# The last 240 columns of a weight quarter as eight loads of three rows, on a single-core decode block

## Chip, cores and metric

One core of a Trainium2 chip runs the whole kernel in one launch. The metric is the device time in microseconds; before the change it is 242.6 us, the median of three runs (242.56 to 242.74).

## What is computed

A decode step of one transformer block with adaptive layer norms, for 4 sequences of one token, D = 512, all in float32. The reference, cut:

```
mod = silu(c) @ w_mod                       # six vectors: sa, ca, ga, sb, cb, gb
h = layernorm(x) * (1 + ca) + sa
q = h @ wq                                  # 512 x 4096, 32 heads of 128
k, v = last 2048 positions of the caches    # 8 groups of kv heads
x = x + ga * (softmax(q k^T / sqrt(128)) v) @ wo
h = layernorm(x) * (1 + cb) + sb
x = x + gb * (silu(h @ w1) * (h @ w3)) @ w2     # 512 x 1792 and 1792 x 512
```

Some 101 MB of caches and weights are read once; the arithmetic for 4 tokens is small beside that.

## The kernel before

**Memory.** An SBUF tensor `ring` has three slots of 128 x 16384 floats (8.39 MB each). Each large input passes through a slot as one DMA of 128 rows of up to 65,536 bytes. All loads are issued by SP (`nc.sync`), in program order, but for `wq`, which ACT issues at the start. The order on SP: `w_mod_a` (the part of w_mod for the first norm, with x and c), `kv_in[0]` to `kv_in[6]` (keys and values of one group each), `wo_mod`, `last_k_wo`, `last_v`, `wo`, `w1`, `w3`, and `w2` in pieces. SP waits ahead of a load until the slot has been read; everything behind the waiting load waits with it.

**Stages.** First x is transposed and normalised, with four contraction quarters of `w_mod_a` (`mod_columns`, line 264), which gives `h` and its transpose `hT` (line 286). Then q (lines 291 to 296): for each half of the heads, four contraction quarters k, four column groups i, 512 columns each; the four column groups write four bands of 32 partitions of one PSUM bank. ACT scales q, PE transposes it, DVE copies it into `qT`. Then `group(g)` (line 332) for the eight groups: scores into four banks, maximum on DVE, exponential on ACT into `p_all` (the tensor `p_sb`), transposes, products with v. After g, the load for g + 3 is issued into the slot that g has left. Output projection, second norm and the feed-forward follow: gate from `w1`, up from `w3`, and `w2` in 14 chunks of 128 rows.

**The end.** `W2_CUTS` cuts w2 into pieces that land one after the other: `[0, 7, 11, 13, 14]` are pieces of 7, 4, 2 and 1 chunks. The chunks of the first piece are multiplied whole (512 columns a product, line 453) into `part`, which ACT copies to `work` (line 454); each later chunk takes eight products of 64 columns (`add_rows`, line 456), and the contents of `work` are added by eight more, ahead of the third piece.

**Waits.** There is no scheduler. Each engine works in program order. `Program.__call__` (line 50) records what each operation touches as boxes, and makes it wait for earlier operations whose boxes overlap. For an SBUF access a box is a range of partitions and a range of columns; the partitions come from lines 28 to 33, the test from lines 61 to 66:

```
    (step, parts), *free = ap.ap
    p0, lo = divmod(ap.offset, row)
    p1, hi = p0 + (parts - 1) * (step // row) + 1, lo + sum((n - 1) * s for s, n in free) + 1
...
                apart = lo >= h or l >= hi or not (writes or wrote)
                if p0 < q1 and q0 < p1 and not (apart and (not psum or other.engine == engine)):
                    if other.engine != engine or other.dma or (wrote and engine != "tensor"):
                        key = other if other.dma else other.engine
                        latest[key] = max(latest.get(key, other), other, key=lambda o: o.index)
```

A step between partitions is not kept: the box runs from the first partition to the last. An operation that touches what an earlier DMA writes waits for that DMA's own semaphore. `emit` (line 77) leaves out waits that the engine knows of already.

The functions as they stand:

Of the kernel before, what the change touches and what calls it, by code (L numbers as in the profile page):

```python
# [8 lines left out]
B, D, HQ, G, SK, DH, W, FF = 4, 512, 32, 8, 8192, 128, 2048, 1792  # L9
P = 128  # L10
R = HQ // G
NT = 4
NC = 4
CHUNKS = [(c, j) for c in range(4) for j in range(4 if c < 2 else 3)]
NF = len(CHUNKS)
W2_CUTS = [0, 7, 11, 13, 14]
EPS = 1e-5
HALF = 8192

# [123 lines left out]
                nc.sync.sem_clear(done)  # L143


def block_kernel(nc, w_mod_a, wq, kv_in, wo_mod, last_k_wo, last_v, wo, w1, w3, w2, out):

# [2 lines left out]
    do = Program(nc)  # L152

    def sb(name, *shape):
        return nc.alloc_sbuf_tensor(name, (P, *shape), F32).ap()
# [5 lines left out]
    slots = [ring[:, n * 2 * HALF : (n + 1) * 2 * HALF] for n in range(3)]  # L161
# [10 lines left out]
    def load(dst, src, cuts=(0, 1), queue="sync"):  # L172
        step = src.shape[1] // cuts[-1]
        for lo, hi in zip(cuts[:-1], cuts[1:]):
            do(queue, "dma_start", dst[:, lo * step : hi * step], src[:, lo * step : hi * step])
        return dst[:, : src.shape[1]]
# [9 lines left out]
    wq_t = load(slots[1], wq, queue="scalar")  # L186
    do("scalar", "preload_act_table_set", "natural_log_exp_and_others")
    kv = [None] * G
    kv[0] = load(slots[2], kv_in[0])

# [1 line left out]
    ident = shifted[:, 4:]  # L194
    do("gpsimd", "memset", shifted, 0.0)
    do("gpsimd", "affine_select", ident, ident, compare_op=ALU.not_equal, fill=1.0, base=0, pattern=[[-1, P]], channel_multiplier=1)
    sc = sb("sc", 4, 32)
    do("gpsimd", "memset", sc, 0.0)

# [36 lines left out]
    xc, sq, h = (sb(n, P) for n in ("xc", "sq", "h"))  # L236
    ss, ln, r0, ve, a, r = (sb(n, 1) for n in ("ss", "ln", "r0", "ve", "a", "r"))
# [19 lines left out]
    def transposed(name):  # L257
        hp = bank()[:, :P]
        do("tensor", "transpose", hp, h, ident)
        hT = sb(name, 4, 32)  # L260
        do("vector", "tensor_copy", hT.rearrange("p j i -> p (j i)"), hp)
        return hT
# [23 lines left out]
    hT = transposed("hT")  # L286
    kv[1] = load(slots[0], kv_in[1])


    work = sb("work", 512)  # L290
    for half in range(2):
        qp = s_ps[half]
        for k in range(4):
            for i in range(4):
                at = ((half * 4 + i) * 4 + k) * 512
                do("tensor", "matmul", qp[32 * i : 32 * i + 32, :], hT[:, k, :], wq_t[:, at : at + 512], start=(k == 0), stop=(k == 3))
    for half in range(2):
        do("scalar", "mul", work, s_ps[half], DH**-0.5)
        qtp = bank()
# [14 lines left out]
            do("tensor", "matmul", a_ps[32 * i : 32 * i + B, :], oT[:, g, i, :], wo_t[g][:, i, :], start=(g == 0), stop=(g == G - 1))  # L314

    mx, nm, ls, l, rl = (sb(n, m) for n, m in (("mx", NT), ("nm", 1), ("ls", NT), ("l", 1), ("rl", 1)))
    p_all = sb("p_sb", NT * 512)
    p_sb = [p_all[:, t * 512 : (t + 1) * 512] for t in range(NT)]
    pT = [sb(f"pT{t}", B, NC, R) for t in range(NT)]
    o_own, o_sum = sb("o_own", NC, P), sb("o_sum", P)  # L320
# [1 line left out]
    def heads_out(g):  # L322

        otp = bank()[:, : R * B]
        if g < G - 1:
            do("tensor", "matmul", otp, o_sum, pick, start=True, stop=True)
        else:
            for c in range(NC):
                do("tensor", "matmul", otp, work[:, c * P : (c + 1) * P], pick_c[:, c].rearrange("p r b -> p (r b)"), start=(c == 0), stop=(c == NC - 1))
        do("vector", "tensor_copy", oT[:, g].rearrange("p r b -> p (r b)"), otp)  # L330
# [62 lines left out]
    w3_t = load(slots[0][:, HALF:], w3)  # L393
    w2_t = load(slots[0][:, :HALF], w2, W2_CUTS)
    heads_out(G - 1)
# [54 lines left out]
    w2_t = w2_t.rearrange("p (n c) -> p n c", n=NF)  # L450
    for n in range(W2_CUTS[1]):
        i = n % 4
        do("tensor", "matmul", part[32 * i : 32 * i + 32, :], hidT[:, n, 4:], w2_t[:, n, :], start=(n < 4), stop=(n + 4 >= W2_CUTS[1]))
    do("scalar", "copy", work, part)
# [6 lines left out]

    for n in range(W2_CUTS[1], NF):
        if n == W2_CUTS[-2]:
            do.mark()
        if n == W2_CUTS[2]:

# [8 lines left out]
def _layout(i):  # L475
    import numpy as np

    def a(t):
        return np.ascontiguousarray(t)

    k = i["A_k_cache"][:, :, SK - W :, :].reshape(B, G, NT, 512, DH)
    v = i["A_v_cache"][:, :, SK - W :, :].reshape(B, G, NT, NC, P, DH)
    wm = i["w_mod"].reshape(4, P, 6, 4, P)
    xc = np.concatenate([i[n].reshape(B, 4, P).transpose(2, 1, 0).reshape(P, 16) for n in ("A_x", "c")], 1)
    w2 = i["B_w2"].reshape(14, P, D)
    wo = a(i["A_wo"].reshape(2, 4, R, P, D).transpose(0, 3, 1, 2, 4)).reshape(2, P, 8192)
    kv = np.concatenate([k.transpose(1, 4, 2, 0, 3).reshape(G, P, 8192), v.transpose(1, 4, 2, 0, 3, 5).reshape(G, P, 8192)], 2)
    return {
        "w_mod_a": np.concatenate([a(wm[:, :, :2].transpose(1, 0, 3, 2, 4)).reshape(P, 4096), xc], 1),
        "wq": a(i["A_wq"].reshape(4, P, G, 512).transpose(1, 2, 0, 3)).reshape(P, 16384),  # L490
        "kv_in": kv[: G - 1],
        "wo_mod": np.concatenate([wo[0], a(wm[:, :, 2:].transpose(1, 0, 3, 2, 4)).reshape(P, 8192)], 1),
        "last_k_wo": np.concatenate([kv[G - 1, :, :8192], wo[1, :, :4096]], 1),
        "last_v": a(kv[G - 1, :, 8192:]),
        "wo": a(wo[1, :, 4096:]),
        "w1": a(i["B_w1"].reshape(4, P, FF).transpose(1, 0, 2)).reshape(P, 4 * FF),
        "w3": a(i["B_w3"].reshape(4, P, FF).transpose(1, 0, 2)).reshape(P, 4 * FF),
        "w2": a(np.stack([w2[4 * j + c] for c, j in CHUNKS], 1)).reshape(P, NF * D),
    }
# [15 lines left out]
```

## Time and profile before

| | |
|---|---|
| median of three runs | 242.6 us |
| span of the profiled execution | 241.1 us |
| PE, DVE, ACT, POOL busy | 146.8, 55.2, 24.0, 2.6 us |
| moved by DMA | 101.38 MB, mean 421 GB/s |
| the chain that ended last | DMA 73%, PE 20% |
| SP waiting, longest | 44.4 us, before the result's store |

The page gives the profiled execution by its span, from the first to the last instruction; the runs' times are 1.5 us longer. The page's chain follows the work that ended last back to what released it. A windows row has the stretch, its length, the busy time of PE, PE's weight loads, DVE, ACT and POOL with the number of instructions, the granted clock, the DMA share and the GB/s. A DMA row gives the time from issue to landing, which includes the time that it stood in the queue.

### The profile page before, as it was taken

How to read it: one execution, taken by the hardware profiler on the slowest of the kernel's cores; microseconds unless marked ns; L12 is line 12 of the kernel's file. 1: busy time of each engine (PE TensorE's matmuls, PEld its weight loads, DVE VectorE, ACT ScalarE, POOL GpSimd, SP SyncE). 2: the span in 40 equal slices, each digit the busy share in tenths (PEclk: the TensorE clock that was granted, in tenths of full speed). 3: DMA queues.
4: the chain of work that ended last, by engine and by line, in shares of the span. 5: the costliest groups of instructions: out<-in, count | busy, mean ns of one | idle time of the engine just before them, and what ended most of it. 6: DMA issues, size and time to landing. Idle time of an engine off the chain costs nothing.

```text
span 241.1 us, 2468 instructions
## 1 busy us (share of the span) xinstructions
PE 146.8 (61%) x1103; PEld 52.8 (22%) x1103; DVE 55.2 (23%) x140; ACT 24.0 (10%) x36; POOL 2.6 (1%) x11
## 2 busy tenths in 40 slices
PE   0000169756782972945767586567296919964876
PEld 0000132213222312201311222221131202422333
DVE  4000220240303124123132124130312014103120
ACT  2000000103003003001200300300300000320100
POOL 3000000000000000000000000000000000000000
PEclk9999997995977799779797589797977997996899
DMA  8999989898989898989999999999999999999993
GB/s 316 414 436 425 500 370 500 351 511 359 511 359 503 370 502 370 489 383 478 391 479 391 478 394 468 402 468 405 457 413 424 435 405 435 407 432 426 416 415 133
DMA packets 2889, 101.38 MB, mean 421 GB/s; under 512 B 448, under 2 KB 448, under 8 KB 704
## 3 DMA queue, kind: packets, MB, share of 16 engines
q1 hardware_dynamic: 2736, 92.85, 89.5%
q10 hardware_dynamic: 144, 8.39, 8.1%
q8 instruction: 8, 0.13, 0.2%
q14 instruction: 1, 0.01, 0.0%
HBM read 101.20 MB, written 0.03 MB: 420 GB/s over the span
## 4 chain that ended last, share of the span: by engine, by line
DMA 73%; PE 20%; DVE 3%; ACT 2%; issue 0%; SPq 0%
DMA ring<-kv_in 30%; DMA ring<-wo_mod 17%; DMA ring<-w 15%; DMA ring<-w_mod_a 11%; PE s_ps L57 8%; PE bank L57 7%; PE o_ps L57 4%; PE a_ps L57 2%; ACT p_sb L57 2%; DVE nm L57 2%; DVE p_sb L57 0%; DVE e L57 0%; DVE sq L57 0%; DVE xc L57 0%; DVE tot L57 0%
## 5 line engine op out<-in xcount | busy, mean ns | idle before, releaser
L57 PE MATMUL s_ps<-ring,qT 128*32 128x512 f32 x256 | 37.0, 731 | 20.2 <-DMA ring<-kv_in 14.7
L57 PE MATMUL bank<-ident,p_sb 128*128 128x128 f32 (+1 forms) x136 | 27.4, 350 | 30.8 <-ACT p_sb L57 30.7
L57 PE MATMUL o_ps<-ring,pT 128*16 128x512 f32 x256 | 37.8, 696 | 0.0
L57 PEld LDWEIGHTS bank<-ident,p_sb 128*128 128x128 f32 (+1 forms) x136 | 19.6, 177 | 51.9 <-ACT p_sb L57 31.7
L57 ACT ACTIVATE p_sb<-s_ps,nm 128x2048 f32<-128x2048 f32 (+1 forms) x11 | 16.5, 1501 | 143.2 <-DVE oT L57 105.2
L57 DVE TENSOR_REDUCE nm<-s_ps 128x1 f32<-128x2048 f32 x7 | 16.0, 2292 | 34.5 <-PE s_ps L57 34.5
L57 DVE COPY pT<-bank 128x64 f32<-128x64 f32 x32 | 7.2, 224 | 56.1 <-PE bank L57 56.1
L57 PEld LDWEIGHTS s_ps<-ring,qT 128*32 128x32 f32 x256 | 9.0, 131 | 47.5 <-issue 20.7
L57 PE MATMUL bank<-ident,xs 128*128 128x128 f32 x1 | 0.5, 473 | 27.8 <-POOL xs L57 27.8
L57 PE MATMUL s_ps<-ring,h2T 128*32 128x512 f32 (+1 forms) x64 | 9.1, 664 | 2.3 <-DMA ring<-w 2.3
L57 PE MATMUL a_ps<-ring,oT 128*4 128x512 f32 x64 | 9.1, 709 | 2.0 <-DMA ring<-wo_mod 2.0
L57 PE MATMUL s_ps<-ring,hT 128*32 128x512 f32 x64 | 8.8, 711 | 0.4 <-DVE hT L57 0.4
L57 PEld LDWEIGHTS o_ps<-ring,pT 128*16 128x16 f32 x256 | 5.4, 98 | 11.6 <-issue 9.2
L57 DVE SCALAR_TENSOR_TENSOR o_own<-o_ps,rl,own 128x512 f32<-128x512 f32 x7 | 5.3, 751 | 11.1 <-PE o_ps L57 11.1
L57 DVE TENSOR_REDUCE o_sum<-o_own 128x128 f32<-128x512 f32 x7 | 7.2, 1029 | 0.2
L57 PE MATMUL bank<-ring,sc 128*32 128x256 f32 (+1 forms) x64 | 7.2, 610 | 0.0
L57 PEld LDWEIGHTS bank<-ident,xs 128*128 128x128 f32 x1 | 0.2, 180 | 27.8 <-POOL xs L57 27.8
L57 DVE TENSOR_SCALAR e<-e 128x16 f32<-128x16 f32 x1 | 0.2, 174 | 23.8 <-ACT e L57 23.8
L57 DVE TENSOR_REDUCE mx<-s_ps 128x1 f32<-128x512 f32 x4 | 2.8, 691 | 7.6 <-PE s_ps L57 7.6
L57 DVE COPY qT<-bank 128x64 f32<-128x64 f32 x8 | 2.2, 277 | 9.8 <-PE bank L57 9.4
L57 PEld LDWEIGHTS s_ps<-ring,h2T 128*32 128x32 f32 x64 | 2.6, 129 | 7.4 <-issue 4.5
L57 PE MATMUL s_ps<-ring,hidT 128*32 128x64 f32 (+1 forms) x126 | 3.7, 262 | 0.3 <-DVE hidT L57 0.3
(93 smaller groups left out, 55.4 us busy)
## 6 DMA issues: line engine op xcount, KB each, us to landing
ring<-w SPq DMA_DIRECT2D x2, 3584.0 KB, 38.3
ring<-last_k_wo SPq DMA_DIRECT2D x1, 6144.0 KB, 30.5
ring<-last_v SPq DMA_DIRECT2D x1, 4096.0 KB, 39.9
ring<-w_mod_a SPq DMA_DIRECT2D x1, 2064.0 KB, 26.6
ring<-wo SPq DMA_DIRECT2D x1, 2048.0 KB, 43.4
ring<-w SPq DMA_DIRECT2D x1, 1792.0 KB, 40.9
ring<-w SPq DMA_DIRECT2D x1, 1024.0 KB, 42.9
ring<-w SPq DMA_DIRECT2D x1, 512.0 KB, 43.7
```

The source lines that it names most:

```text
L57: op = Op(engine, lambda: getattr(getattr(self.nc, engine), method)(*args, **kw), [])
```

## The change

The last 240 columns of the last 512-column block of `wq` (the last contraction quarter of the last column group) are left out of the `wq` load, whose rows shrink from 65,536 to 64,576 bytes. The 128 x 240 values come in instead as 24 rows of 1440 floats, an input `guests`, into partitions 0 to 11 and 32 to 43 of `p_sb`. Eight DMAs on SP carry them, each three rows with a step of four partitions, 5760 bytes a row. POOL first clears 44 partitions of `p_sb`. The eight stand on SP behind `w_mod_a` and ahead of `kv_in[0]`.

To use them, PE makes six copies of columns of `hT` with the rows shifted to partitions 0 to 43 (products of `h` with a part of the identity, into a bank that DVE copies to `hg`), and six products of 240 columns add to the last block of q ahead of its own, which is now 272 columns wide. `p_sb` is allocated earlier for this; its other uses come later.

Apart from that, w2's first piece has 8 chunks instead of 7, the second 3 instead of 4.

The diff, without the host's part beyond the input that it adds:

```
-W2_CUTS = [0, 7, 11, 13, 14]
+W2_CUTS = [0, 8, 11, 13, 14]
+GUESTS = 240
+GUEST_AT = [(0, 0, 12), (12, 0, 12), (24, 0, 8), (64, 0, 12), (76, 0, 12), (84, 4, 12)]
...
     kv = [None] * G
-    kv[0] = load(slots[2], kv_in[0])
...
     do("gpsimd", "affine_select", ident, ident, ...
+
+    p_all = sb("p_sb", NT * 512)
+    do("gpsimd", "memset", p_all[:44], 0.0)
+    guest = p_all[:44, : 6 * GUESTS]
+    for m in range(2):
+        for c in range(4):
+            do("sync", "dma_start", guest[32 * m + c : 32 * m + 12 : 4], guests[12 * m + c : 12 * m + 12 : 4])
+    kv[0] = load(slots[2], kv_in[0])
     sc = sb("sc", 4, 32)
...
     kv[1] = load(slots[0], kv_in[1])
+    hg = p_all[:44, 6 * GUESTS :][:, : 6 * 32]
+    hp = bank()[:44, : 6 * 32]
+    for n, (at, _, _) in enumerate(GUEST_AT):
+        do("tensor", "matmul", hp[:, 32 * n : 32 * n + 32], h[:, at : at + 44], ident[:, 96:], start=True, stop=True)
+    do("vector", "tensor_copy", hg, hp)
...
                 at = ((half * 4 + i) * 4 + k) * 512
-                do("tensor", "matmul", qp[32 * i : 32 * i + 32, :], hT[:, k, :], wq_t[:, at : at + 512], start=(k == 0), stop=(k == 3))
+                n = min(512, 16384 - GUESTS - at)
+                if n < 512:
+                    for c in range(6):
+                        do("tensor", "matmul", qp[96:, n:], hg[:, 32 * c : 32 * c + 32], guest[:, c * GUESTS : (c + 1) * GUESTS], start=False, stop=False)
+                do("tensor", "matmul", qp[32 * i : 32 * i + 32, :n], hT[:, k, :], wq_t[:, at : at + n], start=(k == 0), stop=(k == 3))
...
-    p_all = sb("p_sb", NT * 512)
...
+        "wq": a(wq[:, : 16384 - GUESTS]),
+        "guests": guests.reshape(24, 6 * GUESTS),
```

What stands on SP at the program's start, before. A name with `part0` in brackets is a semaphore; the last part of it is the engine, or the number of the operation if that is a DMA.

```order
L57 DMA ring<-w_mod_a 128x4128 [waits barrier_Pool_Activation_PE_DVE_SP_release]
L57 DMA ring<-kv_in 128x16384
L57 DMA ring<-kv_in 128x16384 [waits part0_22_tensor,part0_22_vector]
L57 DMA ring<-kv_in 128x16384 [waits part0_22_tensor] x5
L57 DMA ring<-wo_mod 128x16384 [waits part0_22_tensor]
```

And after, on the same engine from the same start. The numbers 6 to 13 are the eight guest loads.

```order
L59 DMA ring<-w_mod_a 128x4128 [waits barrier_Pool_Activation_PE_DVE_SP_release]
L59 DMA p_sb<-guests 3x1440 [waits part0_30_gpsimd]
L59 DMA p_sb<-guests 3x1440 [waits part0_30_6]
L59 DMA p_sb<-guests 3x1440 [waits part0_30_7]
L59 DMA p_sb<-guests 3x1440 [waits part0_30_8]
L59 DMA p_sb<-guests 3x1440
L59 DMA p_sb<-guests 3x1440 [waits part0_30_10]
L59 DMA p_sb<-guests 3x1440 [waits part0_30_11]
L59 DMA p_sb<-guests 3x1440 [waits part0_30_12]
L59 DMA ring<-kv_in 128x16384
L59 DMA ring<-kv_in 128x16384 [waits part0_30_tensor,part0_30_vector]
```

The first `kv_in` moved from the second place to the tenth, behind eight loads of which the first waits for POOL and six for the load ahead of them.

On PE, from the transpose of `h` to the start of the first group, before:

```order
L57 MATMUL bank<-ident,h 128x128
L57 MATMUL s_ps<-ring,hT 32x512 x32
L57 MATMUL bank<-ident,work 128x128 x8
L57 MATMUL s_ps<-ring,qT 32x512 x16
L57 MATMUL bank<-ident,p_sb 128x128 x8
```

and after:

```order
L59 MATMUL bank<-ident,h 128x128
L59 MATMUL bank<-ident,h 44x32 x6
L59 MATMUL s_ps<-ring,hT 32x512 x31
L59 MATMUL s_ps<-p_sb 32x240 x6
L59 MATMUL s_ps<-ring,hT 32x272
L59 MATMUL bank<-ident,work 128x128 x8
L59 MATMUL s_ps<-ring,qT 32x512 x16
```

Six small products went in ahead of q, and six of 240 columns ahead of the last one of q.

More of the change, by code (lines that the diff above doesn't have):

```diff
@@ L143, in emit, with block_kernel @@
                 nc.sync.sem_clear(done)
-def block_kernel(nc, w_mod_a, wq, kv_in, wo_mod, last_k_wo, last_v, wo, w1, w3, w2, out):
+def block_kernel(nc, w_mod_a, wq, guests, kv_in, wo_mod, last_k_wo, last_v, wo, w1, w3, w2, out):
     do = Program(nc)
@@ L485, in _layout @@
     w2 = i["B_w2"].reshape(14, P, D)
+    wq = a(i["A_wq"].reshape(4, P, G, 512).transpose(1, 2, 0, 3)).reshape(P, 16384)
+    guests = np.zeros((2, 12, 6, GUESTS), np.float32)
+    for n, (at, lo, hi) in enumerate(GUEST_AT):
+        for m in range(2):
+            guests[m, lo:hi, n] = wq[at + 32 * m + lo : at + 32 * m + hi, 16384 - GUESTS :]
     wo = a(i["A_wo"].reshape(2, 4, R, P, D).transpose(0, 3, 1, 2, 4)).reshape(2, P, 8192)
@@ L489, in _layout @@
         "w_mod_a": np.concatenate([a(wm[:, :, :2].transpose(1, 0, 3, 2, 4)).reshape(P, 4096), xc], 1),
-        "wq": a(i["A_wq"].reshape(4, P, G, 512).transpose(1, 2, 0, 3)).reshape(P, 16384),
+        "wq": a(wq[:, : 16384 - GUESTS]),
+        "guests": guests.reshape(24, 6 * GUESTS),
         "kv_in": kv[: G - 1],
```

## Prediction

> **What bounds the kernel now.** I read the page first: the row of DMA shares in its 40 slices, and the chain that ended last, by engine and by line.
>
> ```profile
> DMA  8999989898989898989999999999999999999993
> DMA 73%; PE 20%; DVE 3%; ACT 2%; issue 0%; SPq 0%
> ```
>
> The 16 DMA engines are 80 to 90% busy or more in every slice but the last, and transfers hold 73% of the chain. The windows view says it in numbers for the main stretch (the last two columns are the DMA share and GB/s).
>
> ```profile
> 27.36:235.00 207.64, 143.03 (x961) 50.35 (x961) 51.82 (x121) 22.18 (x34) 0.21 (x1) 0.84 0.99 429
> ```
>
> A share of 0.99 over 207.64 us leaves no hole. So the time is the bytes at 429 GB/s, plus what lies ahead of the stream and behind it; an idle stretch of the DMA engines anywhere in the middle is added to the end. The chain in order of time (start, length, what) says what lies around it and how deep the queue is filled.
>
> ```profile
> 0.74 26.62 DMA ring<-w_mod_a
> ...
> 85.52 39.92 DMA ring<-kv_in
> ...
> 192.84 37.00 DMA ring<-w
> 229.84 0.04 issue
> 229.88 3.71 PE s_ps L57 x20
> ...
> 235.22 3.80 PE s_ps L57 x138
> ```
>
> A kv_in load asked for at 85.52 lands 39.92 us later, at 125.44, while one such load (8.39 MB) takes 8.39 MB / 429 GB/s = 19.6 us of streaming. So one whole load stands in front of it: each load is asked for some 20 us before its turn. That is the cover for everything in the loop of the groups. There is one place where this cover rests on program order alone: the first kv_in. SP's own timeline shows when it is asked for.
>
> ```profile
> 0.74 0.36 SPq L57 DMA_DIRECT2D ring<-w_mod_a  x1
> 1.15 122.75 SPq L57 DMA_DIRECT2D ring<-kv_in  x7
> ```
>
> Directly behind w_mod_a, at 1.15 us, 0.41 us after it. The windows around the end of the first two loads show when its packets begin (a packet counts in the slice in which it starts, so the GB/s are starts).
>
> ```profile
> 25.00:26.00 1.00, 0.00 (x0) 0.00 (x0) 0.00 (x0) 0.00 (x0) 0.00 (x0) 1.00 0.00 0
> 26.00:26.40 0.40, 0.00 (x0) 0.00 (x0) 0.00 (x0) 0.00 (x0) 0.00 (x0) 1.00 0.00 0
> 26.40:27.10 0.70, 0.00 (x0) 0.00 (x0) 0.00 (x0) 0.00 (x0) 0.00 (x0) 1.00 3.48 1498
> ```
>
> Nothing starts between 25.0 and 26.4; from 26.4 to 27.1 there start 0.70 us x 1498 GB/s = 1.05 MB, which is 16 rows of 65,536 bytes, one for each engine: the first rows of kv_in[0], in the moment in which w_mod_a and wq are done. It had waited in the queue for 25 us.
>
> **The eight guest loads: where the time goes.** They stand on SP between w_mod_a and kv_in[0], and by the order of SP six of them wait for the guest load before them. The cause is in the program's dependency tracking: a box of partitions runs from the first to the last, so rows 0, 4, 8 and rows 1, 5, 9 count as overlapping (0 to 9 and 1 to 10), and a write over a DMA's write waits for that DMA. So SP stops on the first, second and third load of each half, and kv_in[0] is queued behind all of it; each load of the ring that follows is queued behind kv_in[0].
>
> When does the first one land? It first waits for POOL to clear 44 rows of 2048 columns; the nearest row is
>
> ```profile
> L57 POOL MEMSET qT<- 128x1024 f32 x1 | 1.0, 951 | 0.0
> ```
>
> so twice that, 1.9 us, and SP can issue it at some 3.5 us. But it goes into the same queue as w_mod_a, behind that load's rows, and w_mod_a lands at 0.74 + 26.62 = 27.36. Now wq is shorter by 128 x 960 bytes = 0.12 MB, 0.29 us at 429 GB/s, and its rows share the engines with w_mod_a until then: 27.07. The guest row is 5760 bytes at an engine's 429 / 16 = 26.8 GB/s, 0.21 us: the first guest lands at 27.28 us. By then both big loads are over and the engines have nothing else.
>
> From there each wait costs the round trip R of one small DMA on idle engines. The only such DMA in this trace is the result's: the DMA issues (last number: us from issue to landing), and the windows from its issue on SP.
>
> ```profile
> out<-p_sb SPq DMA_DIRECT2D x1, 32.0 KB, 1.5
> ```
>
> ```profile
> 239.56:240.38 0.82, 0.00 (x0) 0.00 (x0) 0.00 (x0) 0.00 (x0) 0.00 (x0) 1.00 0.00 0
> 240.38:240.70 0.32, 0.00 (x0) 0.00 (x0) 0.00 (x0) 0.00 (x0) 0.00 (x0) 1.00 0.49 103
> 0.74:1.72 0.98, 0.00 (x0) 0.00 (x0) 0.75 (x3) 0.56 (x1) 0.75 (x4) 1.00 0.00 0
> ```
>
> 0.82 us from issue to the first packet, 0.32 us of packets, and the rest to 1.5 for the landing. The load of w_mod_a took 0.98 us to its first packet. A guest load has 0.21 us of packets instead of 0.32, but reads from HBM where the result is read from SBUF. From below, R is the result's 1.5 less 0.1 to 0.2 for shorter packets: 1.3. From above, 0.98 to the first packet, twice the 0.32 of packets for a cold read, and 0.4 to land: 2.0, and with a row's latency more, 2.2. I take 1.7, nearer to the result's row, since it is the same kind of issue on the same queue.
>
> The Trainium skill (DMA: Bandwidth & Descriptors, section "Anatomy of one DMA") gives a fixed cost of about 2.0 us for a DMA issued through GpSimd, most of it the receipt of the last write; the result's 1.5 us here is shorter, and no run yet shows a small load. With 2.0 for R the sum below would be 255.3 us.
>
> Now count. After the landing at 27.28, SP issues the second load; its landing lets the third go, whose landing lets the fourth go; the fifth (first of the second half) has no wait and follows the fourth by one issue, 1.15 - 0.74 = 0.41 us. Landings two, three, five, six and seven each pass one R: five round trips. Then the eighth is issued, and kv_in[0] 0.41 us behind it, with its first packet 0.98 us later: 27.28 + 5 x 1.7 + 2 x 0.41 + 0.98 = 37.58 us, where it was 26.4. The stream of all later loads starts **11.2 us** later, and between about 26.5 and 37.5 the DMA engines carry nothing but rows of 5760 bytes.
>
> **What does not change the sum.** The guests' own bytes (24 rows, 0.14 MB) move in that hole, on whichever engines they fall, so neither the 0.29 us that the other engines are relieved of nor extra rows on three engines reach the end of the stream. The relief is already in the 27.28.
>
> The twelve new products lie in the q stage. These are its rows on PE, the start of group 0, the wait for the load behind it, and the page's group of whole-row products.
>
> ```profile
> 36.90 8.77 PE L57 MATMUL s_ps<-ring,hT 128*32 128x512 f32 x64 [0.38 <-DVE hT L57]
> ...
> 48.17 2.35 PE L57 MATMUL s_ps<-ring,qT 128*32 128x512 f32 x20 [0.57 <-DMA ring<-kv_in]
> ```
>
> ```profile
> 67.28 1.07 PE L57 MATMUL s_ps<-ring,qT 128*32 128x512 f32 x8 [2.54 <-DMA ring<-kv_in]
> ```
>
> ```profile
> L57 PE MATMUL s_ps<-ring,qT 128*32 128x512 f32 x256 | 37.0, 731 | 20.2 <-DMA ring<-kv_in 14.7
> ```
>
> Six calls of 32 columns and six of 240 are 24 matrix passes in the trace's count (64 for 32 calls). At most each costs what a 512-column pass takes by itself, 731 ns, times 240/512: 12 x 0.34 = 4.1 us, and the small six under 1 us; at least 12 x 8.77/64 x 240/512 = 0.8 us. Then qT is ready at 49 to 53 us instead of 48. Before, that would have eaten the 2.54 us that PE waited for the next load; now kv_in[0] itself lands near 48 + 11 = 59 us, and the products cost nothing. If the hole did not come, up to 2.5 us of them would be hidden there and the rest made good later, since a load is asked for 20 us ahead.
>
> The copy of the 44 x 192 columns on DVE, the memset on POOL (xs and qT are cleared 1.9 us later, needed after 27 us) and the split of one product into 240 and 272 columns lie under the same cover: nothing. The last stage has one more whole-row product and eight fewer small ones of 64 columns: 14 passes fewer of the 138 that take 3.80 us, at most 0.4 us if they stood on the path and 0 if the last piece of w2 sets it. The last two pieces are as before, so I take 0.
>
> **Sum.** The profiled execution's span is 241.1 us, 1.5 below the median of the runs, 242.6; that difference I keep. 241.1 + 11.2 = 252.3 of span, **253.8 us** of time.
>
> **Rivals.**
> 1. *A dearer round trip.* Each of the five is 2.1 us or more: the three rows of one load go through one engine one after the other (0.4 us more), or the cold read costs more than I took. The result's row speaks against, the lack of any small read in the trace leaves it open. At 2.2: 241.1 + 13.7 + 1.5 = 256.3.
> 2. *The waits are under cover: no loss.* If the guest loads did not stand behind w_mod_a's rows but were served between them, each would take its turn between two wq rows of 65,536 / 26.8 = 2.4 us, and six waits of 1.7 + 2.4 = 4.1 us, begun at 3.5 us, would be over at 28 us, about when the two loads end. Then kv_in[0] is late by 2 us at most. It decides at 3.8 us a wait: below that nothing is lost, and the relief of 0.29 us is left: 242.3 us, not slower. Against it stands that w_mod_a and kv_in[0] are on one queue and that no row of kv_in starts before 26.4 although it was asked for at 1.15: what is behind in this queue waits.
> 3. *The change does only what it says*: no wait is real, eight issues of 0.41 us pass in the 25 us of cover, three engines carry 8 x 0.21 = 1.7 us more and the others 0.29 less. Were the three engines those that end last, the end would come 1.4 us later, 244.0; were they ahead, 0.3 earlier. The order of SP, which shows the six waits, is against this.
>
> The Trainium skill (the same page, section "Queues, rings and completion order") says that on each DMA engine a ring's descriptors are consumed in ring order, which is what the row of zero starts up to 26.4 shows; by that rule rival 2 has no room. The same page's "Why a DMA increments its semaphore by 16 and not by 1" has a three-row load run on the three lowest-numbered engines; no row here shows the engines, and one engine would only raise R.
>
> **How the numbers follow.** The forecast (R between 1.3 and 2.05) has 0.82: 251.8 to 255.6. Rival 1 has 0.11, rival 2 0.03, rival 3 0.04. The range reaches from the forecast's lower bound into rival 1, 251.8 to 256.0, and leaves out rivals 2 and 3, dearer trips than 2.13, and my errors in the fixed terms. No change within 0.2% (0.5 us, about what a measurement of this kernel can tell from none) and faster come only from rivals 2 and 3: 0.04 same, 0.02 faster; slower 0.94.
>
> **What would show it.** In the profile after, slices 5 and 6 of the DMA row (some 25 to 38 us) nearly empty; SP waiting for DMA p_sb<-guests in its own waits, six times, with 1.7 us each in five of them and over 20 us in the first; the issue of kv_in[0] near 36.6; the first PE product of group 0 near 59 instead of 48.17; the chain with guest loads in it. Each later load shifted by the same 11 us, and the stretch from the w3 load's landing to the end as long as now. It is wrong if kv_in[0] starts its packets before 30 us, if the hole is closed again by the end (the shift at the last load smaller than at kv_in[0]), or if R is not between 1.3 and 2.2.

## The result and the profile after

The change makes the kernel slower: **256.93 us**, median of five runs (256.64 to 257.46), against 242.6 us before. The ratio is 1.0596, with a 95% interval of 1.0583 to 1.0609. The direction and the place were forecast; the time lies 0.9 us above the range (251.8 to 256.0). The profiled execution took 257.46 us, of which the span is 256.1.

The page after: DMA shares in 40 slices, and the chain by engine and by line.

```profile
DMA  9999008989989899899899899899899999999993
DMA 69%; PE 22%; DVE 3%; ACT 3%; POOL 1%; issue 1%; SPq 1%; POOLq 0%; ACTq 0%
DMA ring<-kv_in 41%; DMA ring<-w 15%; DMA p_sb<-guests 14%; PE s_ps L59 9%; PE bank L59 6%; PE o_ps L59 6%; DVE nm L59 3%; ACT p_sb L59 3%; PE a_ps L59 1%; POOL p_sb L59 1%; SPq L59 1%; POOL ident L59 0%; DVE p_sb L59 0%; DVE hidT L59 0%; DVE oT L59 0%
```

The fifth and the sixth slice are empty, and a tensor of 0.14 MB holds 14% of the chain. Those 14% include the wait of the first guest load behind w_mod_a; the hole itself is in the windows.

```profile
26.20:27.20 1.00, 0.00 (x0) 0.00 (x0) 0.00 (x0) 0.00 (x0) 0.00 (x0) 1.00 0.06 17
27.20:40.50 13.30, 9.00 (x78) 4.22 (x82) 4.13 (x17) 0.68 (x3) 0.21 (x1) 1.00 0.04 10
40.50:41.50 1.00, 1.00 (x15) 0.28 (x11) 0.00 (x0) 0.20 (x1) 0.00 (x0) 1.00 2.81 983
...
41.50:250.00 208.50, 137.23 (x903) 48.71 (x895) 48.10 (x104) 21.31 (x31) 0.00 (x0) 0.80 0.99 428
```

For 13.3 us the starts come to 10 GB/s; then 0.98 MB start in one microsecond, the first rows of kv_in[0], where before they started between 26.4 and 27.1. From there the stream has no hole, at the rate that it had before (428 against 429 GB/s), so the shift reaches the end: 14.1 us at the first rows, 15.1 at the landing of w3 (244.95 against 229.84), 14.3 between the medians. The profiled execution is the slowest of the five, and in it one of the sixteen first rows comes later than the others (0.98 MB are fifteen). SP's own waits name the cause (total, times, longest).

```profile
SPq L59 <- DMA p_sb<-guests: 30.8, 6, 23.2
```

Six waits, as the order of SP had it. The chain in order of time shows each of them.

```profile
3.24 23.98 DMA p_sb<-guests
27.22 0.02 issue
27.24 2.27 DMA p_sb<-guests
29.51 0.02 issue
29.53 2.09 DMA p_sb<-guests
31.62 0.02 issue
31.64 0.65 SPq L59
32.29 0.04 issue
32.33 2.10 DMA p_sb<-guests
34.42 0.02 issue
34.44 2.14 DMA p_sb<-guests
36.59 0.02 issue
36.60 2.23 DMA p_sb<-guests
38.83 0.02 issue
38.85 0.65 SPq L59
39.50 0.04 issue
39.54 23.83 DMA ring<-kv_in
```

The rows without a word on a wait of SP are its issues: 0.65 us each, at 31.64 (the fourth load, with the fifth behind it) and at 38.85 (the eighth, with kv_in[0] behind it). PE meanwhile finishes q and waits.

```profile
44.59 2.62 PE L59 MATMUL s_ps<-p_sb 44*32 44x240 f32 x12
...
63.51 2.79 PE L59 MATMUL s_ps<-ring,qT 128*32 128x512 f32 x12 [13.79 <-DMA ring<-kv_in]
```

The guest products take 2.62 us, under a wait for kv_in[0] of 13.79.

### The profile page after: what moved, and what is told of

Read it like the earlier page. It is cut to its first block, busy times and chain, and to the rows that moved or that the text cites. A ratio compares the mean times of both kernels' runs of the same rounds, so it can differ in the third digit from the quotient of the medians.

```text
span 256.1 us, 2499 instructions
## 1 busy us (share of the span) xinstructions
PE 150.9 (59%) x1113; PEld 55.4 (22%) x1113; DVE 56.3 (22%) x141; ACT 24.1 (9%) x36; POOL 4.5 (2%) x12
## 4 chain that ended last, share of the span: by engine, by line
DMA 69%; PE 22%; DVE 3%; ACT 3%; POOL 1%; issue 1%; SPq 1%; POOLq 0%; ACTq 0%
DMA ring<-kv_in 41%; DMA ring<-w 15%; DMA p_sb<-guests 14%; PE s_ps L59 9%; PE bank L59 6%; PE o_ps L59 6%; DVE nm L59 3%; ACT p_sb L59 3%; PE a_ps L59 1%; POOL p_sb L59 1%; SPq L59 1%; POOL ident L59 0%; DVE p_sb L59 0%; DVE hidT L59 0%; DVE oT L59 0%
## 5 line engine op out<-in xcount | busy, mean ns | idle before, releaser
L59 PE MATMUL s_ps<-ring,qT 128*32 128x512 f32 x256 | 39.5, 774 | 32.7 <-DMA ring<-kv_in 25.7
L59 PE MATMUL bank<-ident,p_sb 128*128 128x128 f32 (+1 forms) x136 | 28.6, 362 | 30.8 <-ACT p_sb L59 30.7
L59 PEld LDWEIGHTS bank<-ident,p_sb 128*128 128x128 f32 (+1 forms) x136 | 20.7, 185 | 52.4 <-ACT p_sb L59 31.9
L59 PE MATMUL s_ps<-ring,hT 128*32 128x512 f32 (+1 forms) x64 | 7.7, 588 | 0.0
L59 PE MATMUL a_ps<-ring,oT 128*4 128x512 f32 x64 | 7.4, 592 | 0.0
## 6 DMA issues: line engine op xcount, KB each, us to landing
ring<-w_mod_a SPq DMA_DIRECT2D x1, 2064.0 KB, 27.1
```

What stands on the lines that cost most here:

```text
L59: op = Op(engine, lambda: getattr(getattr(self.nc, engine), method)(*args, **kw), [])
```

## Experiments

The theory: the loss is the chain of six waits on SP with kv_in[0] behind it. The main rival: it is the loads or the products themselves, waits or not. A second question opened with the result: why a round trip took 2.1 to 2.3 us where I had 1.7.

**The waits taken away.** The rows of the eight loads are disjoint; the tracking only has to see it. In the changed kernel, one edit in `boxes` (no other SBUF access of the program steps over partitions, so no other wait changes):

```
-    return [(ap.tensor.name, p0, p1, lo, hi, False)]
+    return [(ap.tensor.name, p, p + 1 if step > row else p1, lo, hi, False) for p in (range(p0, p1, step // row) if step > row else [p0])]
```

> The changed kernel with one edit: a box of partitions with a step is one box for each partition, so that the eight guest loads, whose rows are disjoint, no longer wait for each other. If the six waits on SP are the whole loss: kv_in[0] is issued near 3.2 + 8 x 0.65 = 9 us, its first packets start near 26.2 as before, and the time is 242.3 to 242.7 us; 244.0 if the three engines that carry the guests are those that end last. If the loss is the guest loads themselves (0.65 us of issue each, few engines) or the added products, waits or not: 250 us or more.

Measured: 242.11 us (242.05 to 242.27), ratio to before 0.9987 (0.9978 to 0.9996). SP's timeline, and the window of the old hole with the rest of the stream:

```profile
3.23 5.67 SPq L59 DMA_DIRECT2D p_sb<-guests  x8
8.95 0.42 SPq L59 DMA_DIRECT2D ring<-kv_in  x1
```

```profile
26.20:27.50 1.30, 0.00 (x0) 0.00 (x0) 0.00 (x0) 0.00 (x0) 0.00 (x0) 1.00 1.48 630
27.50:235.00 207.50, 144.45 (x989) 51.05 (x993) 52.36 (x122) 22.18 (x34) 0.21 (x1) 0.86 1.00 430
```

All eight loads and all products are there, kv_in[0] is asked for at 8.95, the hole is gone, and the kernel is 0.13% faster than before. The rival falls: nothing but the waits made the change slow. It also shows the cover of the added products at work:

```profile
45.99 2.61 PE L59 MATMUL s_ps<-p_sb 44*32 44x240 f32 x12
...
51.07 2.35 PE L59 MATMUL s_ps<-ring,qT 128*32 128x512 f32 x20
```

Group 0 starts at 51.07 instead of 48.17, 2.9 us later, and the time does not show it.

**A shorter chain of the same loads.**

```
-    for m in range(2):
-        for c in range(4):
+    for c in range(4):
+        for m in range(2):
```

> The changed kernel with the guest loads issued in the other order: the halves alternate (c outside, m inside), so that six still wait but in two chains side by side. If the loss is the length of the chain of waits: two round trips behind the first landing instead of five, with an issue of 0.69 us behind each pair; kv_in[0] is issued near 27.2 + 2 x (2.1 + 0.1) + 2 x 0.69 = 33.0 instead of 39.5, time 250.4 us. If the loss is the eight loads and not how they wait: 256.9 us, unchanged.

Measured: 250.17 us (250.01 to 250.3), ratio 1.0317 (1.0303 to 1.0331). SP:

```profile
3.23 29.46 SPq L59 DMA_DIRECT2D p_sb<-guests  x8
32.73 1.97 SPq L59 DMA_DIRECT2D ring<-kv_in  x2
```

The same eight loads, and six of them again stand behind an earlier one, but in two chains side by side: SP's waits count three (23.9 us in all) where the changed kernel has six, and kv_in[0] is issued 6.81 us earlier than in the changed kernel and the time is 6.76 us shorter. The loss is the length of the chain, microsecond for microsecond.

**The chain moved behind kv_in[0].** One line of the changed kernel moved: `kv[0] = load(slots[2], kv_in[0])` ahead of the guest loads.

> The changed kernel with one line moved: kv_in[0] is issued ahead of the guest loads, which keep their six waits. If the waits cost because of the load that stands behind them on SP, wherever that is: the first guest load now lands behind kv_in[0] near 46.3 us, kv_in[1] is queued behind the chain and starts near 46.3 + 10.9 + 1.4 + 1.05 = 59.6 us where it started at 45.9 before, 13.7 us late, time 256.4 us: the hole only moves. If the loss is of the program's start alone, and later loads have cover: 243 us or less.

Measured: 256.7 us (256.24 to 256.75), ratio 1.0584 (1.0566 to 1.0601). SP:

```profile
1.17 0.42 SPq L59 DMA_DIRECT2D ring<-kv_in  x1
3.23 55.27 SPq L59 DMA_DIRECT2D p_sb<-guests  x8
58.63 7.76 SPq L59 DMA_DIRECT2D ring<-kv_in  x2
```

kv_in[0] comes at its old time, and kv_in[1] is asked for at 58.63 instead of 34.46. The chain only begins when the first guest load gets its turn behind kv_in[0], so the hole moves by one load and costs the same. It is not a matter of the start: whatever is queued behind the chain is late.

**The cut of w2 alone, and the guests without it.** In the kernel before, `W2_CUTS = [0, 8, 11, 13, 14]` alone; and the first experiment with the old cut.

> The kernel before with the other cut of w2 alone (8, 3, 2, 1 chunks). As the prediction has it: the last piece's landing sets the end, no change within 0.2 us, 242.4 to 242.7 us. If eight fewer small products count: 242.2 us.

> As the first run (no waits between the guest loads), with the old cut of w2 (7, 4, 2, 1). If the guests help by relieving thirteen engines by 0.29 us: 242.3 us, and the difference to the first run is the cut's. If they only help together with the cut, since PE's last products are as late as the last landing: 242.6 us.

Measured: the cut alone 242.47 us, ratio 1.0 (0.9991 to 1.0009): no change. The guests with the old cut 242.29 us, 0.999 (0.9982 to 0.9999); this interval and that of the first experiment overlap, so no part of its gain can be given to the cut.

**The chain alone.** The kernel before, with seven loads put ahead of kv_in[0], each over the one before, read by nobody; p_sb is allocated earlier. Five round trips on idle engines, as in the change.

```
+    p_all = sb("p_sb", NT * 512)
+    for n in range(7):
+        do("sync", "dma_start", p_all[:3, :1440], wq[:3, :1440])
     kv[0] = load(slots[2], kv_in[0])
```

> The kernel before, with nothing of the change but a chain of waits: between w_mod_a and kv_in[0] SP issues seven loads of 3 rows of 5760 bytes (columns of wq, into p_sb, read by nobody), each over the one before it, so that each waits for the landing of the one before. Six waits, five of them on idle engines. If a small load's round trip is 2.2 us as in the changed kernel: kv_in[0]'s first packet near 27.5 + 5 x 2.2 + 0.7 + 1.05 = 40.2 us, time 256.5 us. If the chain costs less outside the changed kernel: below 254 us.

Measured: 254.73 us, ratio 1.0505 (1.0489 to 1.0521). With none of the change but a chain of waits, most of the loss is there; but it is 1.8 us less than expected. The group of loads on SP (ns minimum, median, maximum):

```profile
L57 SPq DMA_DIRECT2D p_sb<-wq x7: 239/240/343, 1.2 to 36.9; - x7
```

An issue takes 0.24 us here and 0.65 in the changed kernel. The five trips lie between these two lines of its chain:

```profile
27.59 1.99 DMA p_sb<-wq
...
36.88 0.24 SPq L57
```

A first theory for the length of a trip was that a load has fewer than 16 rows. The next two runs, expected together with the one above, have more:

> As the chain of 3 rows, with 8 rows in each of the seven loads. If a round trip is long because fewer than 16 rows are carried (SP's issue takes 0.65 us instead of 0.33 to 0.43, the first packet comes 1.4 us behind it instead of 0.8 to 1.0): as with 3 rows, 256.5 us. If it shrinks with the number of rows: between 253.3 and 256.5 us.

> As the chain of 3 rows, with 16 rows in each of the seven loads. If the length of the round trip comes from having fewer than 16 rows: about 1.6 us each, as the result's store has it, kv_in[0]'s first packet near 27.5 + 5 x 1.6 + 0.45 + 1.0 = 37.0 us, time 253.3 us. If any small read from HBM takes 2.2 us: 256.5 us.

Measured: 8 rows 256.52 us, ratio 1.0577 (1.0561 to 1.0593); 16 rows 258.01 us, 1.0636 (1.0618 to 1.0654). The chain with 16 rows, likewise:

```profile
28.22 2.28 DMA p_sb<-wq
...
39.84 0.31 SPq L57
```

Sixteen rows are not quicker but slower, above both numbers expected. With 8 rows the number came out as expected, 256.5, but by luck: it was to be that of the 3 rows, and these took 254.73. From issue to issue, five trips long, a trip takes (36.88 - 27.59) / 5 = 1.86 us with 3 rows, 2.12 with 8 and (39.84 - 28.22) / 5 = 2.32 with 16. The theory of too few rows is wrong. What was left that the guests have and the chain of 3 rows has not: the step of four in the partitions written and in the rows read. In the chain of 3 rows, `p_all[:12:4, :1440]` in the first, `wq[:12:4, :1440]` in the second.

> The chain of seven loads of 3 rows again, now into partitions 0, 4 and 8 as the guests have it, where the first chain wrote partitions 0, 1 and 2. In the first chain SP's issue took 0.24 us and a round trip 1.82 us, in the changed kernel 0.65 and 2.2 us. If the step between the partitions written makes the issue longer: 0.65 us an issue, 2.2 us a round trip, 254.7 + 5 x 0.4 + 0.4 = 257.1 us. If not: 254.7 us.

> The chain of seven loads of 3 rows into partitions 0, 1 and 2, now from rows 0, 4 and 8 of wq. If a step in what is read makes the issue longer, as the guests have it too: 257.1 us. If only the partitions written count: 254.7 us.

Measured: a step in what is written 256.29 us, ratio 1.0572 (1.0556 to 1.0588); a step in what is read 254.64 us, 1.0506 (1.049 to 1.0521), as without. The loads on SP with the step in the destination, and then with it in the source:

```profile
L57 SPq DMA_DIRECT2D p_sb<-wq x7: 651/652/797, 1.2 to 38.0; - x7
```

```profile
L57 SPq DMA_DIRECT2D p_sb<-wq x7: 240/241/328, 1.2 to 36.9; - x7
```

The partitions written decide: 0.65 us an issue, as the guests have it, and by the chain below (37.97 - 27.36) / 5 = 2.12 us a trip. The rise of a trip is 0.26 us, less than the 0.41 of the issue, so the time is 0.8 us under what I expected.

```profile
27.36 2.14 DMA p_sb<-wq
...
37.97 0.65 SPq L57
```

The windows of the third of these trips show where the step counts. First without it, then with it, each has a row from the issue to the first packet and one from there to the next issue:

```profile
31.43:32.29 0.86, 0.86 (x16) 0.40 (x12) 0.14 (x1) 0.19 (x1) 0.00 (x0) 1.00 0.00 0
32.29:33.25 0.96, 0.96 (x16) 0.50 (x12) 0.00 (x0) 0.00 (x0) 0.00 (x0) 1.00 0.06 18
```

```profile
31.71:33.13 1.42, 1.42 (x16) 0.59 (x12) 0.00 (x0) 0.00 (x0) 0.00 (x0) 1.00 0.00 0
33.13:33.86 0.73, 0.73 (x12) 0.39 (x8) 0.00 (x0) 0.00 (x0) 0.00 (x0) 1.00 0.08 24
```

With the step the first packet comes 0.56 us later, and the rest of the trip is 0.23 us shorter. Why the rest is shorter no run shows.

**A way without waits that leaves the tracking alone.** The rows can be dealt out so that the boxes do not overlap:

```
-            do("sync", "dma_start", guest[32 * m + c : 32 * m + 12 : 4], guests[12 * m + c : 12 * m + 12 : 4])
+            do("sync", "dma_start", guest[32 * m + 3 * c : 32 * m + 3 * c + 3], guests[12 * m + 3 * c : 12 * m + 3 * c + 3])
```

> The changed kernel with the 24 rows dealt out to the eight loads in another way: three neighbouring partitions a load instead of every fourth, so that the boxes do not overlap and no step is left; the tracking of boxes stays as it is. If waits and step are the whole of the loss: SP issues the eight in 0.24 us each without a wait, kv_in[0] is asked for near 5.7 us, and the time is that of the first run, 242.1 us. If it matters for the stream's end which partitions the three engines write: above 242.5 us.

Measured: 242.72 us (242.44 to 243.41), ratio 1.0011 (1.0002 to 1.002). SP is as expected:

```profile
3.24 2.53 SPq L59 DMA_DIRECT2D p_sb<-guests  x8
5.81 29.36 SPq L59 DMA_DIRECT2D ring<-kv_in  x2
```

No wait, short issues, and the 14 us are back; but the 0.3 us that the first experiment gained are not, and its interval lies above the other's. The two differ in which three rows go into one load and which three partitions it writes, and with it in SP's time for an issue, which is covered in both. That the partitions matter for the end of the stream was the alternative in the expectation; no run here shows by what mechanism, and it stays open. The best kernel of the study is the first experiment, 242.11 us, 0.13% faster than the kernel before.

## Why the prediction was right in direction and wrong in size

- *The place and the mechanism*: right. The hole, the six waits, kv_in[0] behind them, the same rate behind it and no closing of the hole by the end are in the profile: the shift at the landing of w3 is no smaller than at kv_in[0]. From the landing of w3 to the end of the last operation on DVE there are 254.40 + 0.22 - 244.95 = 9.67 us, and 239.30 + 0.22 - 229.84 = 9.68 before (after, then before):

```profile
206.39 38.56 DMA ring<-w
244.95 0.04 issue
...
254.40 0.22 DVE p_sb L59
```

```profile
239.30 0.22 DVE p_sb L57
```

- *The first landing*: 27.28 forecast, 27.22 in the chain. The number is right, in part by luck: I put w_mod_a's landing at 27.07 and 0.21 us for the rows behind it. In the trace w_mod_a lands at 27.8 (0.73 + 27.1), behind the guests; their three rows (58 GB/s x 0.30 us = 17 KB) start well before that, and land over 0.6 us after they start:

```profile
26.30:26.60 0.30, 0.00 (x0) 0.00 (x0) 0.00 (x0) 0.00 (x0) 0.00 (x0) 1.00 0.17 58
```

- *The five round trips, the step that failed.* "I take 1.7, nearer to the result's row, since it is the same kind of issue on the same queue." The chain has 27.24 to 31.64 (two trips) and 32.33 to 38.85 (three): 10.92 us, 2.18 each, where I had 8.5. That term was 2.4 us too small. The runs show what it is made of: 1.86 for three rows into neighbouring partitions, 0.16 above my number; 0.26 more for the step in the partitions; 0.06 is not assigned. Most of what I had too small lies ahead of the packets: 1.42 us from issue to first packet in the trip shown below, where the result's row, on which I leaned, has 0.82. My upper bound of 2.2 held, but trips of 2.1 and more had a chance of 0.11 only. The result's row was the only small DMA in the trace, and it is a store, with no step in its partitions.
- *The two issues in the chain*: 0.41 us each forecast from SP's first two loads, 0.69 each in the chain (31.64 to 32.33, 38.85 to 39.54): 0.56 us too small, for the same step. With the trips: kv_in[0] issued at 39.54 where my terms give 36.60, 2.94 us later; the time is 3.1 us above the forecast.
- *Rival 1*, the dearer trip, is what happened in size, and for another reason than the two that I gave. A row of the trip below took some 0.42 us (1.31 x 16 engines x 0.06 us, for three rows) where I had 0.21, so a dearer read gives some 0.2 us of that trip at most; and the three rows are not served one after the other, since they start within 0.06 us, 1.42 us behind the issue:

```profile
27.24:28.66 1.42, 0.43 (x1) 0.18 (x1) 0.49 (x3) 0.22 (x1) 0.21 (x1) 1.00 0.00 0
28.66:28.72 0.06, 0.05 (x1) 0.00 (x0) 0.06 (x1) 0.00 (x0) 0.00 (x0) 1.00 1.31 288
```

- The Trainium skill (DMA: Bandwidth & Descriptors, section "Anatomy of one DMA") had about 2.0 us as the fixed cost of a DMA issued through GpSimd. The trips measured here on SP's queue, 1.86 to 2.32 us, lie around it, and the 255.3 us that the prediction worked out from it was nearer to the result than the forecast.
- *Rivals 2 and 3*: refuted; the six waits are there, and not under cover. A load behind others in SP's queue waits its turn, which the moved chain shows once more. What the change would be without the waits is 242.1 us, near rival 2's 242.3 with 0.29 us of relief, and not the 244.0 of three engines that end last. That the relief is the reason is not shown: the same rows in neighbouring partitions took 242.72.
- *No charge for the products, the copies and the memset*: right by the first experiment, which has all of them. *No charge for the cut of w2*: right by itself.

## What to carry to other kernels

Where a transfer queue never runs dry, read the order of the issuing engine before the sizes: a wait between two small loads costs every large load behind it one full round trip on idle engines, unless the trips run side by side as in the interleaved order. Look for waits that the program's own tracking invents, as with stepped ranges that are kept as whole ranges. And take the price of a round trip from a run of the very form of load, rows and step, since loads that look alike differ by a quarter here (1.86 to 2.32 us), and the one store, with 1.5 us, was a poor guide.

## What the runs showed of the hardware

- A load of three rows whose partitions are four apart takes SP 0.65 us to issue; into neighbouring partitions it takes 0.24, and a step in the rows read adds nothing (0.24). The trip as a whole takes 2.12 us against 1.86.
- The round trip of a small load on idle engines grows with its rows though each row is 5760 bytes: 1.86, 2.12 and 2.32 us for 3, 8 and 16 rows, with 0.24, 0.27 and 0.31 us of issue in it. In the packets of these traces the first row starts 0.9, 0.9 and 1.0 us behind the issue (means of five trips), and 1.0, 1.2 and 1.4 us pass from there to the next issue, so the growth is mostly behind the first packet.
- Dealing the same 24 rows to the same number of loads by neighbouring instead of every fourth partition moved the time from 242.11 to 242.72 us, with no wait of one load for another in either. No run shows why.
